# Pairing each group's values with the next group's scores in layer A, under a re-fitted order planner

## The chip, the cores and the metric

The kernel runs on one core of a Trainium2 chip. The time is device microseconds from one execution of the whole program. The core's engines each work through their own instruction list in order and meet through semaphores: PE (matrix multiply, with its weight loads shown apart as PEld), DVE (vector), ACT (activations and copies), POOL (masks and the weight loads' DMA issues) and SP (other DMA issues). Three timed runs of the kernel before took 1802.33, 1803.32 and 1803.51 us; the median is 1803.32 us. A change of 0.2% is 3.6 us.

## The reference

Two attention layers stand side by side, each on 2048 positions of width 1024, with 32 heads of 32:

```
qkv = x @ wqkv                                  # both layers
A: each query sees 8 keys, 2 positions apart    # window 8, dilation 2
B: each query sees its last 256 keys            # sliding block
p = softmax(q k / sqrt(32)) ;  o = p v
out = concat(o_A @ wo_A, o_B @ wo_B)
```

All inputs are float32. Nothing is left out or approximated by the change.

## The kernel before

The work is cut into eight units of 512 positions. Units 0 to 3 are layer B ("dense"); units 4 to 7 are layer A, whose positions the host has sorted into even and odd ones, so that the dilation disappears and each query sees its last 8 neighbours. In each unit the 32 heads make eight groups of four heads. Groups are counted through, `hg = 8 u + s`, so layer A has the groups 32 to 63.

Projections are exact to nearly float32: each operand is split into a high fp32r part and the remainder, and three products are summed. In the profile's rows `raw` is a freshly loaded float32 tile, `w`, `x` and `r` are split operands, `g` is the PSUM bank of a projection (three banks), `s` a bank of scores (four banks), `o` the bank of an attention output. The splits are done by `Stream.parts` (L243 to L256): a cast on ACT (L249) or DVE (L252), then subtractions on DVE (L255). Loads into `raw` are issued from POOL's queue (L194), and each waits until the split of an older tile has freed its buffer.

A dense group computes row maxima from a first pass of scores (L1356, L1361), then scores a second time with exponentials (L1441) and masks (L1420), then its values (`o<-pbuf,vbuf`). A group of layer A (`window`, L1145) does this:

- scores: 64 small matmuls of 32 rows by 32 columns, `s<-pbuf` in the rows; they are float32, so the profile counts 128. They read the group's queries and keys from a seat (two seats, L580) that SP's DMAs fill.
- the chain: mask on DVE (L1184), maximum and subtraction (L1194, L1196), exponential on ACT (L1200), sum, reciprocal, product and transpose on DVE (L1208 to L1214), and eight copies on ACT that spread the result into `wide` (L1223, L1226).
- values: 16 or 20 matmuls of 32 columns, `o<-wide,vbuf` (32 or 40 in the profile).

Layer A also forms its output projection and part of its value projection with seven block products in place of eight; the sums of inputs and weights for that are formed on DVE out of line (L1073, L1105), and partial results are gathered by `L979` and `L874`.

What decides the order of all this is a planner inside the kernel's Python. `Clock` holds a modelled time of each engine, of the port that DVE and POOL share, and of DMA transfers. Four lists wait for PE: `a` (small extras), `2` (second scores and values), `1` (first scores and layer A's scores) and `g` (projections, in a fixed sequence). At each step the item with the earliest ready time is issued (L1577 to L1610), and whatever hangs on its end (casts, splits, copies, DMA issues) is issued to the other engines when the model's time reaches it. So a changed number in `Clock` re-deals the instructions of every engine.

One more rule looks after the supply of PE's instructions, which the program gets in chunks of 256. `short(n)` (L299) says that a burst of `n` instructions would outrun what has been fetched; then a projection item is taken in place of the burst, if one is ready:

```
return ck.now < asked[1] + FETCHED and issued[0] + EXTRA + n > asked[0] * CHUNK + ASKED + LEFT
```

Of the kernel before, what the change touches and what calls it, by code (L numbers as in the profile page):

```python
# [22 lines left out]
ASK = 2  # L23
# [8 lines left out]
P_LATE = 1.5  # L32
VPARTS = ((0,4),(4,2),(6,2))
# [19 lines left out]
CW = 1.36  # L53
# [9 lines left out]
class Clock:  # L63
# [7 lines left out]
    MOVE = dict(load=(2.12, 0.14), store=(0.64, 0.4), copy=(1.18, 0.56),  # L71
# [3 lines left out]
    def __init__(self):  # L75
        self.free = dict(pe=0.0, act=0.0, dve=0.0, pool=0.0, sp=0.0)
        self.port = dict(dve=0.0, pool=0.0)
        self.later, self.lands, self.busy = [], [], []
        self.n = 0
# [17 lines left out]
    def use(self, eng, dur, *ready, port=False):  # L97
        end = self.free[eng] = self.ends(eng, dur, *ready, port=port)
        if eng == "pool" or port:
            self.port[eng] = end  # L100
        return end + self.SEEN[eng]

    def issue(self, eng, kind, *ready):
        start = max((self.free[eng],) + ready) + (0.28 if eng == "pool" else 0.0)
        self.free[eng] = start + self.HOLD[eng]
        return self.move(start + self.LEAD[eng], *self.MOVE[kind])

# [18 lines left out]
    def move(self, t, dur, tail):  # L126

        busy = self.busy = [x for x in self.busy if x[1] > self.now - 20.0]
        i = 0
        while i < len(busy):  # L130
            if busy[i][1] <= t or busy[i][0] < t:
                t = max(t, busy[i][1])
            elif busy[i][0] - t >= dur:
                break
            else:
                t = busy[i][1]
            i += 1
        busy.insert(i, (t, t + dur))
        return t + dur + tail
# [10 lines left out]
class Stream:  # L150
# [14 lines left out]
    def load_to(self, n):  # L165
        while not self.loaded:
# [4 lines left out]
            for n, (i, h) in enumerate(FIRST):  # L171
                raw, t = self.raw[i]
                ap = self.items[i][1]
                queue, took = (self.nc.scalar, self.ck.load) if n in BY_ACT else (self.nc.sync, self.ck.copy)
# [90 lines left out]
def kernel(ctx, tc, xs, wqk, wv, wo, outs, units):  # L265
# [33 lines left out]
    def short(n):  # L299
        return ck.now < asked[1] + FETCHED and issued[0] + EXTRA + n > asked[0] * CHUNK + ASKED + LEFT  # L300
# [27 lines left out]
    for k in ("stack", "v", "o", "ot", "out", "nat", "second", "clear", "scores", "s", "t", "vs", "vw", "vd"):  # L328
        done[k] = {}
# [210 lines left out]
    def qk_items(u, s):  # L540
# [14 lines left out]
        def evac_window(t, ps, bank):  # L555
# [5 lines left out]
            else:  # L561
# [5 lines left out]
                if u + 1 < U and not units[u + 1][3]:  # L567
                    ck.defer(e + 1.0, lambda: (nc.vector.memset(tails[:, s, :], 0.0), ck.use("dve", 0.08, ck.now)))
# [70 lines left out]
        for t in range(2):  # L639
# [15 lines left out]
            def run(k, t=t, h=h):  # L655
# [12 lines left out]
                if k == ASK and t == 0 and u > DU and kinds[:1] == ["x"] and st.split >= where["qk", u, s, 1]:  # L668
                    st.split_to(where["qk", u, s, 1] + 1)
# [30 lines left out]
    def v_items(u, part):  # L700
# [25 lines left out]
        def run(r, n, k, b):  # L726
# [418 lines left out]
    def window(u, s):  # L1145
# [100 lines left out]
        return [Item(scores_ready, scores, CW, 256)], [Item(values_ready, values, C3 + 0.9, 16 * len(kbs))]  # L1246
# [404 lines left out]
```

## Time and profile before

| | |
|---|---|
| median of three runs | 1803.32 us |
| the profiled execution | 1802.41 us, of which the span of instructions is 1800.7 us |
| mean granted PE clock | 0.999 |
| PE busy | 1775.3 us (99%) |
| DVE busy | 1297.4 us (72%) |
| ACT busy | 940.3 us (52%) |
| POOL busy | 413.7 us (23%) |
| DMA | 324.58 MB, mean 180 GB/s |

A row of the timeline gives the start, the length and the number of instructions of a run of equal ones; in brackets stands the idle time ahead of it and what ended that. A row of the waits gives, for an engine and line, the total, the number and the longest of its idle stretches by what released them; "issue" means that the instruction waited for nothing else that the profile shows. A matmul's row lasts longer than the step to the next one, since matmuls overlap; the step is what counts, and it is read from the starts.

### The profile page before, as it was taken

What the parts mean: (1) busy time and instruction counts of PE and PEld (TensorE: products, weight loads), DVE (VectorE), ACT (ScalarE), POOL (GpSimd) and SP (SyncE); (2) the same over time, 40 slices, a digit from 0 to 9 for tenths busy, and PEclk for the clock granted to TensorE, in tenths of its full rate; (3) what the DMA queues carried; (4) which work ended last, traced back from release to release, by engine and by line L of the source; (5) the groups of instructions that cost most, each with busy time, mean ns of one, the idle gap of its engine ahead of it and who ended that gap; (6) DMA issues with size and microseconds to landing.
All of it is one profiled execution on the core that took longest, in us unless ns stands there. A gap on an engine that the chain in (4) does not pass through costs nothing.

```text
span 1800.7 us, 38453 instructions
## 1 busy us (share of the span) xinstructions
PE 1775.3 (99%) x14496; PEld 1439.2 (80%) x14496; DVE 1297.4 (72%) x2887; ACT 940.3 (52%) x2336; POOL 413.7 (23%) x952
## 2 busy tenths in 40 slices
PE   9999999999999999999999999999999999999999
PEld 7787777888777888778788778877888787778887
DVE  6777876768867769867678566756666768688866
ACT  4565566555656565655655444534454435355442
POOL 3222323222242222332223400110011101001120
PEclk9999999999999999999999999999999999999999
DMA  8354664644645555455546265665466558758984
GB/s 245 112 152 135 185 167 135 171 138 138 185 141 172 152 131 167 144 159 148 141 124 174 84 190 180 213 211 187 160 212 204 192 177 285 265 181 273 350 287 146
DMA packets 154794, 324.58 MB, mean 180 GB/s; under 512 B 18032, under 2 KB 58992, under 8 KB 154608
## 3 DMA queue, kind: packets, MB, share of 16 engines
q0 software_dynamic: 45792, 166.74, 29.8%
q1 hardware_dynamic: 98736, 137.02, 26.6%
q10 hardware_dynamic: 10080, 18.35, 2.7%
q8 instruction: 115, 1.88, 0.4%
q14 instruction: 71, 0.58, 0.1%
HBM read 201.33 MB, written 53.48 MB: 142 GB/s over the span
## 4 chain that ended last, share of the span: by engine, by line
PE 87%; DVE 5%; issue 3%; DMA 2%; ACT 2%; POOL 1%; DVEq 0%; POOLq 0%; ACTq 0%
PE g L297 68%; PE s L297 13%; PE o L297 6%; DMA raw<-xs 1%; DVE w L255 1%; DVE x L255 1%; ACT s L1361 0%; DVE band L1212 0%; DMA raw<-wv 0%; DVE sm L1208 0%; DVE band L1184 0%; ACT w L249 0%; DMA raw<-wqk 0%; DVE w L252 0%; DMA qst<-nat 0%
## 5 line engine op out<-in xcount | busy, mean ns | idle before, releaser
L297 PE MATMUL g<-x,w 128*128 128x512 f32 x3552 | 878.9, 393 | 5.0 <-DVE x L255 3.9
L297 PEld LDWEIGHTS g<-x,w 128*128 128x128 f32 x3552 | 654.8, 188 | 135.2 <-issue 6.6
L255 DVE TENSOR_TENSOR w<-raw,w 128x512 fp32r<-128x512 f32 x510 | 334.3, 697 | 48.5 <-ACT w L249 42.4
L1361 ACT ACTIVATE s<-s,nm 128x384 f32<-128x384 f32 (+2 forms) x512 | 274.4, 537 | 108.2 <-DVE nm L1356 101.7
L1356 DVE CUSTOM_DVE_ANT_0 s<-s,mask_d 128x384 f32<-128x384 f32 (+2 forms) x512 | 261.7, 553 | 91.7 <-PE s L297 91.4
L297 PE MATMUL g<-w,x 128*128 128x256 f32 (+1 forms) x1728 | 307.9, 327 | 2.4 <-DVE w L255 1.5
L1420 POOL TENSOR_SCALAR_AFFINE_SELECT pbuf<-pbuf 128x128 f32<-128x128 f32 (+1 forms) x603 | 218.4, 390 | 317.9 <-ACT pbuf L1441 315.9
L297 PEld LDWEIGHTS g<-w,x 128*128 128x128 f32 x1728 | 255.2, 190 | 28.0 <-DVE w L255 2.8
L297 PE MATMUL g<-r,w 128*128 128x512 f32 x960 | 239.0, 393 | 1.7 <-issue 1.2
L1441 ACT ACTIVATE pbuf<-s 128x384 f32<-128x384 f32 (+2 forms) x480 | 203.1, 505 | 64.2 <-PE s L297 62.0
L297 PEld LDWEIGHTS g<-r,w 128*128 128x128 f32 x960 | 177.2, 188 | 37.2 <-issue 2.0
L194 POOL DMA_DIRECT2D raw<-wqk x126 | 68.6, 544 | 407.4 <-DVE w L255 256.8
L297 PEld LDWEIGHTS s<-qst,kst 128*128 128x128 f32 x704 | 113.4, 188 | 42.6 <-ACT s L1361 16.8
L297 PE MATMUL s<-kst,qst 96*128 96x384 f32 (+2 forms) x512 | 142.6, 342 | 0.9 <-ACT s L1361 0.7
L297 PE MATMUL s<-qst,kst 128*128 128x256 f32 (+2 forms) x704 | 137.0, 302 | 4.0 <-ACT s L1361 3.2
L252 DVE CAST w<-raw 128x1024 fp32r<-128x1024 f32 x173 | 119.8, 692 | 19.3 <-PE g L297 9.0
L249 ACT CAST w<-raw 128x1024 fp32r<-128x1024 f32 (+1 forms) x83 | 85.8, 1038 | 71.1 <-PE g L297 29.7
L297 PEld LDWEIGHTS s<-kst,qst 96*128 96x128 f32 x512 | 93.6, 189 | 26.3 <-issue 4.4
L1361 ACT ACTIVATION_READ_ACCUMULATOR s<-s,nm 128x1 f32 x512 | 105.3, 206 | 0.0
L1223 ACT COPY wide<-band 32x512 f32<-32x512 f32 x128 | 79.0, 617 | 31.0 <-DVE band L1214 29.4
L297 PE MATMUL o<-pbuf,vbuf 128*32 128x384 f32 (+2 forms) x1408 | 91.2, 388 | 0.0
L597 ACT ACTIVATE nat<-g 128x512 fp32r<-128x512 f32 x64 | 38.3, 598 | 98.2 <-PE g L297 89.0
(90 smaller groups left out, 1432.1 us busy)
## 6 DMA issues: line engine op xcount, KB each, us to landing
raw<-wqk POOLq DMA_DIRECT2D x126, 512.0 KB, 4.6
raw<-wv POOLq DMA_DIRECT2D x60, 512.0 KB, 5.0
qst<-nat SPq DMA_DIRECT2D x96, 256.0 KB, 5.7
kst<-nat SPq DMA_DIRECT2D x96, 256.0 KB, 5.7
raw<-wo POOLq DMA_DIRECT2D x44, 512.0 KB, 4.4
raw<-xs POOLq DMA_DIRECT2D x28, 512.0 KB, 4.5
outs<-ost ACTq DMA_DIRECT2D x38, 256.0 KB, 3.1
kst<-halo SPq DMA_DIRECT2D x72, 128.0 KB, 4.5
```

The costliest lines, as they stand in the source:

```text
L194: (self.nc.scalar if early else self.nc.gpsimd).dma_start(raw if len(ap.shape) == 2 else raw.rearrange("p (a b) -> p a b", a=2), ap)
L249: nc.scalar.copy(t[:, 0, :], raw)
L252: nc.vector.tensor_copy(t[:, 0, :], raw)
L255: nc.vector.tensor_tensor(t[:, 1, c:c + 512], raw[:, c:c + 512], t[:, 0, c:c + 512].bitcast(F32), op=ALU.subtract)
L297: nc.tensor.matmul(out, left, right, **k)
L597: nc.scalar.activation(hl[:, 0, :], ps, AF.Copy, scale=sc)
L1223: nc.scalar.copy(diag[r:r + 32, :, :, c:c + 32], turned[r:r + 32, :, :, 1, :])
L1356: nc.vector.tensor_tensor_reduce(ps[:, :n], ps[:, :n], mask[:, cut:full], scale=-1.0, scalar=BIG, op0=ALU.add, op1=ALU.min, accum_out=nm)
L1361: nc.scalar.activation(ps[:, :n], ps[:, :n], AF.Exp, bias=nm, scale=-1.0, accum_out=sm)
L1420: nc.gpsimd.affine_select(w, w, pattern=[[0, m], [step, n]], compare_op=ALU.is_ge, fill=0.0, base=base, channel_multiplier=chan)
L1441: nc.scalar.activation(w, ps[:, :pack * n].rearrange("p (j n) -> p j n", j=pack), AF.Exp)
```

## The change

The change has six parts.

1. In layer A, for the groups 33 to 49 (`PAIRED = 50`), a group's scores are held until the previous group's spread probabilities are modelled as there (plus `P_LATE`), and the values of the previous group are held until those scores have been issued. So the two stand together on PE. The scores count, for `short`, with the values' instructions too.
2. `short` also limits a burst once the last asked chunk has come: then one more chunk counts as there.
3. The model of the shared port keeps the stretches in which DVE holds it, and POOL waits only if it starts inside one.
4. The model of DMA keeps two streams, one for loads from POOL's queue and one for the rest. They share the bandwidth where they overlap, and a load takes 1.5 + 0.76 in place of 2.12 + 0.14.
5. In the start, a loop variable had the name of the function's argument, so that eight items were wanted at once; it has another name now, and six are wanted.
6. Smaller: the eight clears of `tails` go from DVE to POOL; the split of a unit's second key weights ahead of its inputs is also made for the dense units 2 and 3; in the wide value items two weight tiles are wanted ahead in place of one.

```diff
+PAIRED = 50
...
-    MOVE = dict(load=(2.12, 0.14), store=(0.64, 0.4), copy=(1.18, 0.56),
+    MOVE = dict(load=(1.5, 0.76), store=(0.64, 0.4), copy=(1.18, 0.56),
...
         if eng == "pool":
-            t = max(t + 0.06, self.port["dve"])
-        elif port:
-            t = max(t, self.port["pool"])
-        return t
+            t += 0.06
+            return next((e for s, e in self.held if s <= t < e), t)
+        return max(t, self.port) if port else t
...
-    def move(self, t, dur, tail):
...
+    def move(self, eng, t, dur, tail):
+
+        mine, other = self.moves[eng == "pool"], self.moves[eng != "pool"]
+        t = begin = max(t, mine[-1][1] if mine else 0.0)
+        for s, e in other:
+            if e <= t:
+                continue
+            n = max(s - t, 0.0)
+            if n >= dur:
+                break
+            t, dur = t + n, dur - n
+            n = min((e - t) / 2, dur)
+            t, dur = t + 2 * n, dur - n
+            if not dur:
+                break
+        mine.append((begin, t + dur))
...
-            for n, (i, h) in enumerate(FIRST):
+            for turn, (i, h) in enumerate(FIRST):
...
     def short(n):
-        return ck.now < asked[1] + FETCHED and issued[0] + EXTRA + n > asked[0] * CHUNK + ASKED + LEFT
+        there = asked[0] * CHUNK + ASKED + LEFT + (0 if ck.now < asked[1] + FETCHED else CHUNK)
+        return issued[0] + EXTRA + n > there
...
-                    ck.defer(e + 1.0, lambda: (nc.vector.memset(tails[:, s, :], 0.0), ck.use("dve", 0.08, ck.now)))
+                    ck.defer(e + 1.0, lambda: (nc.gpsimd.memset(tails[:, s, :], 0.0), ck.use("pool", 0.08, ck.now)))
...
-                if k == ASK and t == 0 and u > DU and kinds[:1] == ["x"] and st.split >= where["qk", u, s, 1]:
+                if k == ASK and t == 0 and u > 1 and kinds[:1] == ["x"] and st.split >= where["qk", u, s, 1]:
...
-                    ahead(item_of(n + 1))
+                    ahead(item_of(min(n + 2, 3)))
...
         def scores_ready():
-            return latest(rs.empty(), done["stack"].get((u, s)),
+            if last_dense + 1 < hg < PAIRED and hg - 1 not in done["p"]:
+                return None
+            return latest(rs.empty(), done["stack"].get((u, s)), done["p"][hg - 1] + P_LATE if last_dense + 1 < hg < PAIRED else 0.0,
...
-                h["p"] = ck.use("act", 0.31, e)
+                done["p"][hg] = h["p"] = ck.use("act", 0.31, e)
...
         def values_ready():
+            if hg + 1 < PAIRED and hg + 1 not in done["scores"]:
+                return None
...
-        return [Item(scores_ready, scores, CW, 256)], [Item(values_ready, values, C3 + 0.9, 16 * len(kbs))]
+        return [Item(scores_ready, scores, CW, 256 + (16 * len(kbs) if hg < PAIRED else 0))], [Item(values_ready, values, C3 + 0.9, 16 * len(kbs))]
```

Matmuls and DMA issues are the same in number and kind as before; a few casts, copies and masks go from one engine to another. Where they all stand is another matter. On PE, at the start of layer A, before (`s<-pbuf` are scores, `o<-wide,vbuf` values, `g` projections):

```order
L297 MATMUL s<-pbuf 32x40 x64
L297 MATMUL g<-x,w 128x512 x27
L297 MATMUL s<-pbuf 32x40 x64
L297 MATMUL g<-x,w 128x512 x18
L297 MATMUL g<-r,w 128x512 x15
L297 MATMUL o<-wide,vbuf_131 32x136 x12
L297 MATMUL o<-wide,vbuf_131 32x128 x4
L297 MATMUL s<-pbuf 32x40 x64
```

and in the changed kernel, from its second group of layer A on:

```order
L303 MATMUL s<-pbuf 32x40 x64
L303 MATMUL o<-wide,vbuf_127 32x136 x12
L303 MATMUL o<-wide,vbuf_127 32x128 x4
L303 MATMUL g<-x,w 128x512 x69
L303 MATMUL g<-w,x 128x256 x42
L303 MATMUL s<-pbuf 32x40 x64
L303 MATMUL o<-wide,vbuf_127 32x136 x12
L303 MATMUL o<-wide,vbuf_127 32x128 x4
```

Scores and values touch at 4 places of the 32 groups before, and at 18 now; between one such pair and the next stand 57 to 114 projection matmuls.

On POOL, at the program's start, before (the selects build the masks):

```order
L194 DMA raw<-wqk 128x1024 x2
L463 MEMSET keep_d 128x128
L464 ISA
L464 AFFINE_SELECT ident<-keep_d 128x128
L467 MEMSET pick 32x16
L469 AFFINE_SELECT pick<-pick 32x16 x2
```

and now, with the end of the masks and what follows them:

```order
L462 MEMSET keep_f 128x128
L464 AFFINE_SELECT keep_f<-keep_f 128x128
L462 MEMSET keep_d 128x128
L464 AFFINE_SELECT keep_d<-keep_d 128x128
L200 DMA raw<-wqk 128x1024 x2
L200 DMA raw<-wv 128x2x512 x5
```

The masks have gone ahead of the first two weight loads; the five value-weight loads, which stood behind the masks in the kernel before too, follow at once.

On DVE, around the splits of the last unit's inputs (`x<-raw,x`, two instructions for each of four loads), before:

```order
L255 TENSOR_TENSOR x<-raw,x 128x512 x2
L979 TENSOR_TENSOR r<-g,r 128x512 x2
L1208 TENSOR_REDUCE sm<-band 128x16
L1210 RECIPROCAL sm<-sm 128x16
L1212 TENSOR_TENSOR band<-band,sm 128x16x40
L1214 STREAM_TRANSPOSE band<-band 128x1024
L1184 TENSOR_TENSOR band<-s,near 128x4x40 x4
L255 TENSOR_TENSOR x<-raw,x 128x512 x2
```

and now:

```order
L261 TENSOR_TENSOR x<-raw,x 128x512 x2
L1217 TENSOR_REDUCE sm<-band 128x16
L1219 RECIPROCAL sm<-sm 128x16
L1221 TENSOR_TENSOR band<-band,sm 128x16x40
L1223 STREAM_TRANSPOSE band<-band 128x1024
L986 TENSOR_TENSOR r<-g,r 128x512 x2
L261 TENSOR_TENSOR x<-raw,x 128x512 x2
L986 TENSOR_TENSOR r<-g,r 128x512 x2
L261 TENSOR_TENSOR x<-raw,x 128x512 x2
L1193 TENSOR_TENSOR band<-s,near 128x4x40 x4
```

The chain of one group has gone from between the third and the fourth pair of splits to between the second and the third, and the next group's masks (L1184, now L1193) have gone behind the fourth.

More of the change, by code (lines that the diff above doesn't have):

```diff
@@ L76, in __init__ @@
         self.free = dict(pe=0.0, act=0.0, dve=0.0, pool=0.0, sp=0.0)
-        self.port = dict(dve=0.0, pool=0.0)
-        self.later, self.lands, self.busy = [], [], []
+        self.port, self.held = 0.0, []
+        self.later, self.lands, self.moves = [], [], [[], []]
         self.n = 0
@@ L98, in use @@
         end = self.free[eng] = self.ends(eng, dur, *ready, port=port)
-        if eng == "pool" or port:
-            self.port[eng] = end
+        if eng == "pool":
+            self.port = end
+        elif port:
+            self.held = [x for x in self.held if x[1] > self.now - 5.0] + [(end - dur, end)]
         return end + self.SEEN[eng]
@@ L105, in issue @@
         self.free[eng] = start + self.HOLD[eng]
-        return self.move(start + self.LEAD[eng], *self.MOVE[kind])
+        return self.move(eng, start + self.LEAD[eng], *self.MOVE[kind])
     def copy(self, kind, *ready):
@@ L170, in load_to @@
                 self.raw[3 + i] = raw, [None, None]
-            for n, (i, h) in enumerate(FIRST):
+            for turn, (i, h) in enumerate(FIRST):
                 raw, t = self.raw[i]
                 ap = self.items[i][1]
-                queue, took = (self.nc.scalar, self.ck.load) if n in BY_ACT else (self.nc.sync, self.ck.copy)
+                queue, took = (self.nc.scalar, self.ck.load) if turn in BY_ACT else (self.nc.sync, self.ck.copy)
                 if h is None:
@@ L327 @@
     done = {}
-    for k in ("stack", "v", "o", "ot", "out", "nat", "second", "clear", "scores", "s", "t", "vs", "vw", "vd"):
+    for k in ("stack", "v", "o", "ot", "out", "nat", "second", "clear", "scores", "s", "t", "vs", "vw", "vd", "p"):
         done[k] = {}
```

11 lines of the change are left out of this document (1 added, 10 removed).

## The prediction

> **What bounds the kernel now.** I read the page first, for who is busy.
>
> ```profile
> span 1800.7 us, 38453 instructions
> PE 1775.3 (99%) x14496; PEld 1439.2 (80%) x14496; DVE 1297.4 (72%) x2887; ACT 940.3 (52%) x2336; POOL 413.7 (23%) x952
> ```
>
> PE is the bound from end to end. The change adds no matmul and takes none away, so it can move the time in two ways only: by PE's idle stretches, and by the dearer steps where PE goes from 128-column to 32-column matmuls and back. So the second view is PE's own waits.
>
> ```profile
> PE s L297 <- ACT s L1361: 4.6, 7, 1.0
> PE g L297 <- DVE x L255: 3.9, 3, 2.8
> PE g L297 <- DVE w L255: 3.0, 6, 0.8
> PE s L297 <- issue: 2.2, 1, 2.2
> PE g L297 <- DVE w L252: 1.5, 2, 1.0
> PE s L297 <- DVE qst L1569: 1.5, 1, 1.5
> PE g L297 <- issue: 1.2, 1, 1.2
> PE s L297 <- DVE hl L1382: 0.6, 2, 0.3
> PE s L297 <- DVE qst L1396: 0.6, 2, 0.4
> ```
>
> These nine rows make 19.1 us, 1.1% of the span (smaller ones are left out). That is about all that a new order can win; what it can lose has no such ceiling. Most of these waits are single events, so I looked each up in the timeline and then asked the built order whether the instructions that made it still stand so.
>
> **The change part by part.** *Pairing.* Two stretches of PE's timeline, first values alone, then values right behind scores:
>
> ```profile
> 1156.53 10.50 PE L297 MATMUL g<-x,w 128*128 128x512 f32 x45
> 1166.87 1.52 PE L297 MATMUL g<-w,x 128*128 128x512 f32 x6
> 1168.32 1.12 PE L297 MATMUL o<-wide,vbuf 128*32 128x136 f32 x32
> 1169.37 0.50 PE L297 MATMUL g<-w,x 128*128 128x512 f32 x1
> ...
> 1177.06 1.32 PE L297 MATMUL s<-pbuf 32*32 32x40 f32 x128
> 1178.31 1.12 PE L297 MATMUL o<-wide,vbuf 128*32 128x136 f32 x32
> 1179.36 0.96 PE L297 MATMUL g<-w,x 128*128 128x512 f32 x3
> ```
>
> A projection steps in (1166.87 - 1156.53) / 45 = 0.23 us. The six ahead of the lone values took 1168.32 - 1166.87 = 1.45, so the last of them, which leads into 32-column work, took 1.45 - 5 x 0.23 = 0.30, with the rounding up to 0.32: 0.09 dearer at most. The values' own 1.05 is the same alone (1169.37 - 1168.32) and behind scores (1179.36 - 1178.31). So a pair saves one entry and nothing else. Scores and values touch at 18 places now and touched at 4: 14 x 0.09 = **-1.3 us**; the ends are that and, if a pair has a cost of its own, 0. The new wait is the planner's and stands in no queue: PE does projections meanwhile. What it holds up is the seat that SP's DMAs fill for the next group but one; the pairs stand 57 to 114 projections apart (13 to 26 us), which leaves that room. Behind the last values of the built order stand 537 matmuls (123 us), so a layer A that ends a little later costs nothing. I cost this at zero; without that cover it would be a wait of PE for the seat, as long as the slip.
>
> *The supply of instructions.* The page's row of the queue that brings them (packets, MB, share), and PE's timeline at the longest wait on "issue":
>
> ```profile
> q8 instruction: 115, 1.88, 0.4%
> 1046.76 1.32 PE L297 MATMUL s<-pbuf 32*32 32x40 f32 x128
> 1054.36 1.24 PE L297 MATMUL s<-pbuf 32*32 32x40 f32 x119
> 1057.76 0.28 PE L297 MATMUL s<-pbuf 32*32 32x40 f32 x9 [2.17 <-issue]
> ```
>
> 1.88 MB in 115 packets are 16 KB each, one for about 256 of PE's 29,000 instructions (each matmul has its weight load). A projection phase needs one packet in 29 us, but a group of scores uses 256 instructions in 1.2 us. The second group here came 7.6 us behind the first and ran dry after 119 of 128. The "issue" rows above make 3.4 us. A pair uses 320 or 336 instructions at once, which is worse, but no pair now follows another within 13 us, and `short` refuses more. The groups from 50 on still stand freely, so I keep 0.6: **-2.8 us**. The ends are -3.4 and, if pairs run dry, the first rival.
>
> *The start.* POOL's first rows, DVE's wait for the value weights, DVE beside the longest select, and PE's first use of the first weight load:
>
> ```profile
> 8.70 0.68 POOL L194 DMA_DIRECT2D raw<-wqk  x1 [8.19 <-DVE x L255]
> 10.74 3.83 POOL L464 TENSOR_SCALAR_AFFINE_SELECT ident<-keep_d 128x128 fp32r<-128x128 f32 x1
> 22.93 2.19 POOL L194 DMA_DIRECT2D raw<-wv  x3
> 30.55 0.69 DVE L252 CAST w<-raw 128x1024 fp32r<-128x1024 f32 x1 [7.10 <-DMA raw<-wv]
> 10.72 1.29 DVE L255 TENSOR_TENSOR r<-pbuf,r 128x512 fp32r<-128x512 f32 x2
> 12.52 1.29 DVE L255 TENSOR_TENSOR r<-pbuf,r 128x512 fp32r<-128x512 f32 x2
> 19.69 2.88 PE L297 MATMUL g<-x,w 128*128 128x512 f32 x12
> ```
>
> POOL's list was blocked for 8.2 us by a load whose buffer was not free, the masks came behind it, and the value weights were issued at 22.93; PE then waited 0.6 (DVE w L252) and 0.8 (DVE w L255, its longest) for them. With the masks first (some 12.4 us of work, from just ahead of 10.74 to 22.93), the loads go out from about 13 us, two for the first weights and then the value weights, some 8 us earlier than now. Those 1.4 us go. In turn the first weight load moves from 8.70 to about 13 and its data, first needed at 19.69 by the projection in the last row, come 4 us later, and masks run beside DVE's first splits; for both I put 0.3: **-1.1 us**, with ends -1.4 and +1.5 (the wait moved to the first load, as long as the one removed).
>
> [...] In the rows above DVE's two-input splits kept their 0.6 us each inside POOL's 3.83 us select, so here it was at most POOL that waited. [...]
>
> *The dense units.* PE's waits between 440 and 970 us, and one of them in the timeline:
>
> ```profile
> PE s L297 <- ACT s L1361: 1.8, 3, 0.6
> PE s L297 <- DVE hl L1382: 0.6, 2, 0.3
> PE g L297 <- DVE r L1320: 0.4, 2, 0.2
> ...
> 453.14 0.82 PE L297 MATMUL s<-qst,kst 128*128 128x128 f32 x4 [0.61 <-ACT s L1361]
> ```
>
> Two or three times each, so one event for each unit from the second on. At 453.14 nine score matmuls stood in a row, filling five banks where there are four, so the last pairs wait for the exponential of the first. In the built order such rows of five banks are cut by three projections (0.7 us), which is more than the 0.61. I take 2.2 of these 2.8 us off. In the first unit the other 2.8 us of the same row (4.6 - 1.8) come from runs of scores with nothing to put between; the new order has the same kind of runs there, a little looser: 1.0 off. Together **-3.2 us**, ends -5.6 and 0.
>
> *The last unit's inputs.* DVE around PE's longest wait (2.8, DVE x L255):
>
> ```profile
> 1511.59 1.28 DVE L979 TENSOR_TENSOR r<-g,r 128x512 f32<-128x512 f32 x2
> 1514.76 1.29 DVE L255 TENSOR_TENSOR x<-raw,x 128x512 fp32r<-128x512 f32 x2 [1.88 <-ACT x L249]
> 1517.17 0.81 DVE L1208 TENSOR_REDUCE sm<-band 128x16 f32<-128x640 f32 x1
> 1521.22 1.27 DVE L255 TENSOR_TENSOR x<-raw,x 128x512 fp32r<-128x512 f32 x2
> ```
>
> From 1517.17 to 1521.22 DVE did a group's chain and the next one's masks, 4.05 us, while PE waited for the splits behind them. In the built order the chain stands a load earlier, where DVE had 1.88 us to spare, and the masks behind the splits. So the splits come 1.88 + 0.9 (the masks) earlier: **-2.4 us** of 2.8, ends -2.8 and 0.
>
> *A weight behind sums.* Also on DVE:
>
> ```profile
> 1431.59 1.79 DVE L1073 TENSOR_TENSOR r<-r 128x256 f32<-128x256 f32 x4
> 1433.30 0.69 DVE L252 CAST w<-raw 128x1024 fp32r<-128x1024 f32 x1
> ```
>
> PE waited 1.0 (DVE w L252) and 0.8 (DVE w L255) for this cast and the splits behind it. In the built order the cast and its splits stand ahead of the four sums, 1.7 us earlier: **-1.7 us**, ends -1.8 and 0.
>
> *What is late next.* The clear of `tails` on POOL and the other small edits move single instructions of 0.1 us on engines with room, and cost nothing. But each engine's order is dealt anew, and waits that no row of before shows will come. I put them at a third of what the last three terms give back, 7.3 / 3 = **+2.4 us**; the ends are 0 and all 7.3, since the same hand could be dealt again.
>
> The sum is -1.3 - 1.1 - 2.8 - 3.2 - 2.4 - 1.7 + 2.4 = -10.1 us. The profiled execution took 1802.4 us, its span and 1.7 us around it; 1802.4 - 10.1 = 1792.3. It lay 0.9 under the median of the three runs, so I predict 1793.2 us. With all good ends it is -1.4 - 1.4 - 3.4 - 5.6 - 2.8 - 1.8 = -16.4, so 1787; with all bad ones 1.5 + 7.3 = +8.8, so 1812.
>
> **The rivals.** *Pairs run dry* (slower). Each of the 17 pairs holds up to 336 instructions; if a pair begins before the packet asked for during the last one is there, PE stands for some 2.2 us, as at 1057.76. For it: the count of instructions that `short` goes by was fitted to the old order. Against it: the spacing. Five stalling pairs eat the forecast's gain; ten give 1793.2 + 10 x 2.2 = 1815 us.
>
> *The same hand again* (no change). What is gained in the places that I looked up is lost in others: the dense, input and weight terms give nothing in all, and the new waits come on top, -1.3 - 1.1 - 2.8 + 2.4 = -2.8, so 1800.5 us, 0.16% under before. For it: all those waits are accidents of an order, and the model that deals has changed, not what the kernel needs. Against it: they can be named, and each stands better now.
>
> [...]
>
> **How the numbers follow.** The three runs before lie within 0.07%; 0.2%, 3.6 us, is about what can be told from no change. Forecast 0.70; masks hold the start 0.04; same hand 0.12; pairs run dry 0.10; 0.04 for a worse deal that I don't see. So faster 0.74, same 0.12, slower 0.14. The forecast's own range is 1787 to 1799. To leave out no more than 2 in 10, the range takes in the same hand: 1787 to 1803.
>
> **What would show it.** Pairing: no wait on "issue" over 1 us before group 50, values right behind scores with a 1.25 us step. The start: value weights issued near 14 us and no PE wait near 31 us. Dense: the waits for ACT s L1361 fall from 4.6 us to about 2.4. Inputs: the longest wait for DVE x L255 under 1 us. PE's waits in all near 11 us. I am wrong if "issue" rows grow, if a wait for x or w over 2 us stands at another unit's start, or if the gap between first and last PE instruction shrinks by less than 6 us.

## The result, and the profile after

The change made the kernel slower: median 1810.22 us in eight runs, beside 1803.67 us for the kernel before in eight; the ratio is 1.0033, with a 95% interval of 1.0019 to 1.0046. The profiled execution took 1809.79 us. The page of the changed kernel begins:

```profile
span 1808.1 us, 38431 instructions
PE 1777.1 (98%) x14496; PEld 1441.7 (80%) x14496; DVE 1300.2 (72%) x2871; ACT 935.3 (52%) x2326; POOL 422.7 (23%) x978
q8 instruction: 115, 1.88, 0.4%
```

The span is 7.4 us longer with as many matmuls. PE's waits, over the whole span:

```profile
PE s L303 <- ACT s L1372: 6.7, 9, 2.1
PE g L303 <- DVE band L881: 5.6, 2, 3.9
PE g L303 <- DVE w L261: 4.5, 9, 1.3
PE o L303 <- issue: 1.9, 2, 1.5
PE s L303 <- DVE qst L1580: 1.5, 1, 1.5
PE s L303 <- ACT ln L1385: 1.1, 1, 1.1
...
PE g L303 <- DVE x L261: 0.2, 1, 0.2
```

Some rows did what was forecast: the wait for x is 0.2 us where it was 3.9, the longest wait for a weight's second split (w L261) is one of 1.3 us, "issue" in all is 1.9. Others grew: the wait for ACT's exponentials (6.7, was 4.6), and a new one of 5.6 us for the adds of the output products (L881, which was L874 and 0.3 us before).

For a sum by stage, each step from one PE matmul to the next was set against the usual one: the 20th percentile of such a pair of shapes over all kernels of this study. What lies above it is called lost time; it holds the waits, the half-clock steps (below) and all small delays, which are most of it: PE's named waits are 20.7 us in all before and 25.0 after.

| us | before | after | difference |
|---|---|---|---|
| usual steps in all (fewer entries into 32-column work) | 1621.9 | 1620.3 | -1.6 |
| lost: start, 0 to 40 us | 6.2 | 4.2 | -2.0 |
| lost: the rest of the first unit, to 440 | 37.3 | 38.9 | +1.6 |
| lost: second to fourth dense unit, 440 to 1040 | 47.8 | 55.2 | +7.4 |
| lost: layer A, 1040 to 1640 | 77.7 | 69.3 | -8.4 |
| lost: end of layer A and what follows | 3.7 | 14.3 | +10.6 |
| first to last matmul | 1794.7 | 1802.1 | +7.4 |

(The rows are rounded.) So layer A, the start and the entries gained 12.0 us. The dense units, the first one included, for which the forecast had -3.2, and the end, for which it had nothing of its own, lost 19.6.

**The dense units.** PE's waits from 440 to 1040 us, where the kernel before had 2.8 us in all:

```profile
PE s L303 <- ACT s L1372: 4.5, 5, 2.1
PE g L303 <- DVE w L261: 1.1, 1, 1.1
PE s L303 <- ACT ln L1385: 1.1, 1, 1.1
PE s L303 <- DVE hl L1393: 0.6, 1, 0.6
```

The longest of them, on three engines (PE first, then DVE, then ACT):

```profile
965.16 2.23 PE L303 MATMUL g<-x,w 128*128 128x512 f32 x9
969.53 1.01 PE L303 MATMUL s<-kst,qst 96*128 96x384 f32 x2 [2.15 <-ACT s L1372]
...
965.42 0.43 DVE L258 CAST x<-raw 128x512 fp32r<-128x512 f32 x1 [4.29 <-PE g L303]
965.89 0.69 DVE L261 TENSOR_TENSOR x<-raw,x 128x512 fp32r<-128x512 f32 x1
...
967.56 0.68 DVE L1331 TENSOR_TENSOR r<-o,r 128x512 fp32r<-128x512 f32 x1
968.16 0.56 DVE L1367 CUSTOM_DVE_ANT_0 s<-s,mask_d 128x384 f32<-128x384 f32 x1
...
968.81 0.56 ACT L1372 ACTIVATE s<-s,nm 128x384 f32<-128x384 f32 x1 [2.86 <-DVE nm L1367]
```

DVE stood for 4.29 us at a cast that waited for PE's projections to be done with its tile. The row maxima (L1367) were queued behind it, ACT's exponential waited for them, and PE for the bank. No engine was short of time; the order was wrong by a few instructions.

**The end of layer A.** DVE, then PE, then the stretch in which the granted clock fell (columns: stretch, length, busy time and count of PE, PEld, DVE, ACT, POOL, PE clock, DMA share, GB/s):

```profile
1651.97 1.01 DVE L1193 TENSOR_TENSOR band<-s,near 128x160 f32<-128x160 f32 x4
1657.87 2.87 DVE L1112 TENSOR_TENSOR r<-r 128x512 f32<-128x512 f32 x4 [4.89 <-DMA r<-od]
1660.65 0.68 DVE L881 TENSOR_TENSOR ost<-g,r 128x512 f32<-128x512 f32 x1
...
1674.96 0.69 DVE L881 TENSOR_TENSOR band<-g,r 128x512 f32<-128x512 f32 x1 [2.90 <-DMA outs<-band]
...
1666.08 5.82 PE L303 MATMUL g<-x,w 128*128 128x512 f32 x24 [1.67 <-DVE band L881]
1675.80 5.09 PE L303 MATMUL g<-x,w 128*128 128x512 f32 x15 [3.90 <-DVE band L881]
1680.82 1.18 PE L303 MATMUL o<-wide,vbuf 128*32 128x8 f32 x40
```

```profile
1660.00:1680.00 20.00, 13.87 (x52) 10.33 (x51) 16.83 (x27) 9.60 (x16) 2.12 (x4) 0.91 0.92 321
```

DVE stood 4.89 us at the sums for the output products (L1112), whose loads had not landed; everything behind them came late: the chain of layer A's last group, the splits, and the adds (L881) that free PE's three banks. One of those adds then waited 2.90 us for the store of an earlier add, itself among the late ones. PE waited 1.67 and 3.90 us, and its granted clock was 0.50 for 3.41 us from 1675.42: the 15 projections from 1675.80 to 1680.82 took 0.33 us each, not 0.23. In all PE waited 8.1 us behind 1640 us, where the kernel before had 0.3: 6.1 for the adds (0.56 of it for one with another output, `ost`), 1.5 on "issue" and 0.5 for a DMA.

**Layer A.** A pair on PE, and PE's two waits on issue:

```profile
1155.24 10.39 PE L303 MATMUL g<-x,w 128*128 128x512 f32 x45
1165.56 1.32 PE L303 MATMUL s<-pbuf 32*32 32x40 f32 x128
1166.80 1.12 PE L303 MATMUL o<-wide,vbuf 128*32 128x136 f32 x32
1167.86 0.96 PE L303 MATMUL g<-x,w 128*128 128x512 f32 x3
...
1501.29 0.42 PE L303 MATMUL o<-wide,vbuf 128*32 128x128 f32 x6 [0.40 <-issue]
1651.36 0.41 PE L303 MATMUL o<-wide,vbuf 128*32 128x128 f32 x4 [1.50 <-issue]
```

Scores step in 1.24 us, values in 1.06, and no pair ran dry. The two rows on "issue" are of groups behind the 50th, which still stand freely.

**The start.** The select that took 3.83 us before, and POOL's first loads, where before the value weights were issued at 22.93:

```profile
1.09 0.29 POOL L471 TENSOR_SCALAR_AFFINE_SELECT ident<-keep_d 128x128 fp32r<-128x128 f32 x1
9.98 1.23 POOL L200 DMA_DIRECT2D raw<-wqk  x2
11.29 0.72 POOL L200 DMA_DIRECT2D raw<-wv  x1
16.28 0.73 POOL L200 DMA_DIRECT2D raw<-wv  x1 [4.28 <-DVE w L261]
```

PE no longer waits near 31 us. The select took 0.29 us here, ahead of DVE's splits, and 3.83 us in the kernel before, beside them, while the splits kept their 0.6 us each. So it was POOL that had waited, and the masks were done by 9.98 us, not by about 13. The port that the two engines share is a term of the planner's model; of it the traces show such lengths and no more.

### The profile page after: what moved, and what is told of

Same layout as the page of the kernel before. It is cut to its first block, busy times and chain, and to the rows that moved or that the text cites. A ratio compares the mean times of both kernels' runs of the same rounds, so it can differ in the third digit from the quotient of the medians.

```text
span 1808.1 us, 38431 instructions
## 1 busy us (share of the span) xinstructions
PE 1777.1 (98%) x14496; PEld 1441.7 (80%) x14496; DVE 1300.2 (72%) x2871; ACT 935.3 (52%) x2326; POOL 422.7 (23%) x978
## 4 chain that ended last, share of the span: by engine, by line
PE 82%; DVE 7%; DMA 6%; issue 2%; ACT 2%; POOL 1%; SPq 0%; ACTq 0%; DVEq 0%; POOLq 0%
PE g L303 64%; PE s L303 12%; PE o L303 6%; DMA raw<-xs 2%; DVE w L261 2%; DMA r<-od 1%; DVE s L1367 1%; DVE x L261 1%; ACT s L1372 1%; POOL pbuf L1431 1%; DMA raw<-tv 1%; DVE w L258 1%; DMA sd<-r 1%; DMA outs<-band 0%; DMA od<-r 0%
## 5 line engine op out<-in xcount | busy, mean ns | idle before, releaser
L303 PEld LDWEIGHTS g<-x,w 128*128 128x128 f32 x3552 | 658.7, 188 | 136.4 <-issue 10.1
L261 DVE TENSOR_TENSOR w<-raw,w 128x512 fp32r<-128x512 f32 x510 | 337.0, 702 | 42.6 <-ACT w L255 36.4
L1367 DVE CUSTOM_DVE_ANT_0 s<-s,mask_d 128x384 f32<-128x384 f32 (+2 forms) x512 | 261.7, 555 | 118.3 <-PE s L303 117.5
L1431 POOL TENSOR_SCALAR_AFFINE_SELECT pbuf<-pbuf 128x128 f32<-128x128 f32 (+1 forms) x621 | 230.1, 398 | 269.4 <-ACT pbuf L1452 267.0
L1193 DVE TENSOR_TENSOR band<-s,near 128x160 f32<-128x160 f32 x128 | 32.5, 317 | 90.0 <-PE s L303 90.0
L200 POOL DMA_DIRECT2D raw<-wv x60 | 38.7, 645 | 233.9 <-DVE w L261 122.0
```

The lines of the kernel that those rows point to most:

```text
L200: (self.nc.scalar if early else self.nc.gpsimd).dma_start(raw if len(ap.shape) == 2 else raw.rearrange("p (a b) -> p a b", a=2), ap)
L261: nc.vector.tensor_tensor(t[:, 1, c:c + 512], raw[:, c:c + 512], t[:, 0, c:c + 512].bitcast(F32), op=ALU.subtract)
L303: nc.tensor.matmul(out, left, right, **k)
L1193: nc.vector.tensor_tensor(p64()[:, j, :, 24:], banks[j][0][:, :160].rearrange("p (b c) -> p b c", b=4), m, op=ALU.add)
L1367: nc.vector.tensor_tensor_reduce(ps[:, :n], ps[:, :n], mask[:, cut:full], scale=-1.0, scalar=BIG, op0=ALU.add, op1=ALU.min, accum_out=nm)
L1431: nc.gpsimd.affine_select(w, w, pattern=[[0, m], [step, n]], compare_op=ALU.is_ge, fill=0.0, base=base, channel_multiplier=chan)
```

## Experiments

Each kernel is the kernel before with some of the change's parts: P pairing, L the new limit for supply, R the renamed variable, C the clears on POOL, T two tiles ahead, E the early splits of units 2 and 3, Mp the model of the port, Mt the model of transfers. "All" is the changed kernel. The ratio is to the kernel before, measured beside it. The kernel before had medians from 1803.15 to 1804.35 us on these occasions. The columns by stage and "half", the number of windows of 3.41 us that PE ran at half clock, are from the one profiled execution, which lies up to 4.5 us from the median.

| kernel | median us | ratio, 95% | lost: start | to 440 | dense | layer A | end | half |
|---|---|---|---|---|---|---|---|---|
| before | 1803.67 | | 6.2 | 37.3 | 47.8 | 77.7 | 3.7 | 1 |
| all | 1810.22 | 1.0019-1.0046 | 4.2 | 38.9 | 55.2 | 69.3 | 14.3 | 1 |
| all but P | 1815.72 | 1.0053-1.0086 | 4.2 | 39.8 | 54.2 | 75.1 | 16.1 | 5 |
| P | 1806.26 | 1.0009-1.0029 | 6.3 | 38.9 | 47.5 | 79.9 | 7.7 | 2 |
| P L R C T E | 1807.40 | 1.0007-1.0027 | 4.6 | 37.6 | 59.5 | 72.4 | 6.8 | 5 |
| Mp Mt | 1824.20 | 1.0095-1.0131 | 6.9 | 39.7 | 59.7 | 72.0 | 15.3 | 6 |
| all, sums later | 1806.89 | 1.0014-1.0035 | 4.2 | 38.9 | 54.5 | 71.7 | 8.7 | 1 |
| Mt | 1827.06 | 1.0107-1.0138 | 9.9 | 41.2 | 55.2 | 78.1 | 14.1 | 6 |
| Mp | 1817.30 | 1.0056-1.0091 | 7.4 | 39.4 | 58.1 | 72.3 | 15.1 | 5 |
| P L R C T | 1801.12 | 0.9973-0.9991 | 4.6 | 37.4 | 52.6 | 75.8 | 3.7 | 2 |
| all but E | 1819.58 | 1.0073-1.0101 | 4.3 | 39.6 | 56.9 | 71.6 | 14.9 | 4 |
| before, nudged up | 1810.09 | 1.0024-1.0049 | 6.2 | 42.3 | 54.4 | 72.1 | 7.3 | 4 |
| before, nudged down | 1816.84 | 1.0062-1.0089 | 5.4 | 45.5 | 54.9 | 75.8 | 6.0 | 4 |
| all, nudged up | 1810.26 | 1.0029-1.0055 | 4.1 | 41.4 | 55.6 | 70.0 | 10.5 | 3 |
| nudged up, P | 1824.86 | 1.0097-1.0128 | 5.5 | 41.1 | 55.9 | 81.8 | 10.1 | 5 |
| nudged down, P | 1820.31 | 1.0070-1.0100 | 8.2 | 44.6 | 55.1 | 76.1 | 7.2 | 3 |
| P L | 1803.36 | 0.9984-1.0005 | 6.2 | 38.9 | 47.5 | 74.6 | 6.4 | 2 |
| P L R C T, nudged up | 1809.84 | 1.0022-1.0042 | 4.8 | 38.8 | 55.2 | 74.0 | 5.5 | 2 |
| P L T | 1802.97 | 0.9992-1.0010 | 5.7 | 37.4 | 53.8 | 72.6 | 3.8 | 1 |
| R | 1800.91 | 0.9977-1.0000 | 4.6 | 37.4 | 47.5 | 77.5 | 4.2 | 1 |

**The large parts, taken out and alone.** The pairing out of the changed kernel, and alone in the kernel before:

```diff
+            if last_dense + 1 < hg < PAIRED and hg - 1 not in done["p"]:
+                return None
...
+            if hg + 1 < PAIRED and hg + 1 not in done["scores"]:
+                return None
...
-        return [Item(scores_ready, scores, CW, 256)], [Item(values_ready, values, C3 + 0.9, 16 * len(kbs))]
+        return [Item(scores_ready, scores, CW, 256 + (16 * len(kbs) if hg < PAIRED else 0))], [Item(values_ready, values, C3 + 0.9, 16 * len(kbs))]
```

> The changed kernel with all its parts but the pairing (the two conditions, and the values counted with the scores for the supply of instructions, are out). If the pairing cost the time (theory 1: it ties every group to the chain of the one before, layer A comes out later and its end runs into the output products), the loss goes: about 1799 to 1802 us, PE's waits for L881 near the end under 1 us. If the new model of port and DMA cost it (theory 2: it re-deals the dense units and the end of layer A worse), the loss stays and the 1.3 us of the pairing and some of the supply come on top: 1810 to 1814 us, waits between 440 and 1040 us about 7 us as in the changed kernel. If no single part cost it (theory 3: every change of a number deals all engines anew, and the parts do not add), it lies anywhere from 1797 to 1812.

> The kernel before with the pairing alone. Theory 1: about 1808 to 1812 us, slower than before by the loss seen. Theory 2: faster than before by the pairing's 1.3 us and by the 3.4 us of waits on issue, 1798 to 1801 us. Theory 3: neither is bound to hold; the dense units, which stand ahead of every pair, should keep their waits to the last row, and the difference should lie behind 980 us alone.

Then the models of port and transfers as before in the changed kernel, and alone in the kernel before:

```diff
-    MOVE = dict(load=(2.12, 0.14), store=(0.64, 0.4), copy=(1.18, 0.56),
+    MOVE = dict(load=(1.5, 0.76), store=(0.64, 0.4), copy=(1.18, 0.56),
...
-            t = max(t + 0.06, self.port["dve"])
+            t += 0.06
+            return next((e for s, e in self.held if s <= t < e), t)
...
-    def move(self, t, dur, tail):
+    def move(self, eng, t, dur, tail):
```

> The changed kernel with the model of port and DMA as before (and the load at 2.12 + 0.14), all else kept. Theory 1: still about 1808 to 1812 us. Theory 2: 1796 to 1801 us, PE's waits from 440 to 1040 us back at about 2.8 us. Theory 3: any of 1797 to 1812, with losses in places that stand in no other kernel.

> The kernel before with the new model of port and DMA alone (and the load at 1.5 + 0.76). Theory 1: 1799 to 1804 us. Theory 2: 1808 to 1814 us, with about 7 us of PE's waits from 440 to 1040 us and a wait for L874 (the adds of the output products) of some 5 us near the end. Theory 3: a time in between, and waits in other places than in the changed kernel.

Measured: 1815.72, 1806.26, 1807.40 and 1824.20 us. The first theory, that the pairing cost it, falls: without it the changed kernel is 5.5 us slower still. The second holds for the direction only: the models cost 2.8 us on top of the other parts (1810.22 - 1807.40) and 19.9 alone. And the parts do not add: the pairing saves 5.5 us in one place and costs 1.9 in the other. Alone it also ran dry, which it did not in the changed kernel. PE's waits on "issue" behind 1040 us with the pairing alone:

```profile
PE g L298 <- issue: 2.1, 3, 1.0
PE o L298 <- issue: 2.7, 3, 1.5
PE s L298 <- issue: 0.9, 2, 0.6
```

**The end of layer A alone.** The sums are dealt to DVE later, which can move nothing ahead of 1640 us:

```diff
-        ck.defer(e + (BG_EARLY if key == "s" and who[0] < PAIRS[0] else BG_SLACK), add)
+        ck.defer(e + (BG_EARLY if key == "s" else BG_SLACK), add)
```

> The changed kernel; only the sums that feed the last unit's output products are put into DVE's order 8 us behind their loads' modelled landing, in place of 1.5 us. Nothing ahead of about 1640 us can move. If the model of the transfers lets the loads land too early (theory 2), so that DVE stands in front of the sums while the adds that free PE's banks queue behind it, the two waits for L881 (5.6 us) fall under 2 us and with them the half-clock stretch at 1676 us: 1803 to 1806 us. If the transfers are simply full there, L881 still waits, for the stores of its own band: 1809 to 1811 us.

Measured 1806.89 us, 3.3 less than the changed kernel; the end's lost time went from 14.3 to 8.7. Between 1640 us and the end PE waited in one place for those adds, and the half-clock stretch was gone (the 21 projections step in 0.24 us):

```profile
1673.40 5.02 PE L303 MATMUL g<-x,w 128*128 128x512 f32 x21 [2.78 <-DVE band L881]
1678.35 1.18 PE L303 MATMUL o<-wide,vbuf 128*32 128x8 f32 x40
```

So the sums that came too early made about half of the end's loss (5.6 of 10.6 us). Of the 5.0 us left, this trace's waits behind 1640 us name 4.4: the 2.78 above, 1.35 on "issue" and 0.30 for a DMA. The add that PE waited 2.78 us for stood in DVE's list behind the next sums (2.86 us) and the chain of the last group, and DVE worked there without a break from 1664.85 to 1673.17 us. The wait was to fall under 2 us, and the time is 0.9 us over the range that the theory gave: the theory holds for a part.

**The two models apart.** With the two numbers of the load, the transfers alone; then the port alone.

> The kernel before with the new model of transfers alone (two streams, and the load at 1.5 + 0.76). If the loss of the new models lies in the transfers: 1812 to 1824 us, with waits for L874 near the end of 4 us or more and a wait for DMA kst<-nat at the start. If it lies in the port: 1802 to 1807 us.

> The kernel before with the new model of the port alone. If the loss of the new models lies in the transfers: 1801 to 1806 us, L874 waits under 1 us. If it lies in the port (POOL's work modelled as starting earlier, so masks and loads put where they can't run yet): 1812 to 1824 us, with PE waits in the dense units of 6 us or more.

Measured 1827.06 and 1817.30 us: the question was put wrongly, since both lose. But the wait for the adds at the end tells them apart. From 1640 us on, with the transfers alone and with the port alone:

```profile
PE g L301 <- DVE band L878: 3.5, 2, 3.0
```

```profile
PE s L298 <- issue: 4.5, 1, 4.5
PE g L298 <- DVE band L875: 0.6, 1, 0.6
```

All six kernels dealt with the new model of transfers wait 3.9 to 6.1 us in all for these adds (the seventh, with the sums later, 2.8); of the others, and of the kernel before, none waits over 0.6 us. That wait therefore goes with the model of transfers. The port's kernel lost as much at the end by another accident, a group of scores that ran dry for 4.49 us.

**The early splits.** The changed kernel under the old models, without the splits ahead of units 2 and 3, and then the changed kernel without them:

```diff
-                if k == ASK and t == 0 and u > 1 and kinds[:1] == ["x"] and st.split >= where["qk", u, s, 1]:
+                if k == ASK and t == 0 and u > DU and kinds[:1] == ["x"] and st.split >= where["qk", u, s, 1]:
```

> The kernel before with the pairing, the new limit for supply, the renamed variable, the clears on POOL and the two tiles ahead; the models of port and transfers, and the splits ahead of units 2 and 3, as before. If those early splits cost the 5.7 us for hl L1388 between 440 and 1040 us that the kernel with the old models showed (and the four half-clock windows with them): 1796 to 1800 us, which is faster than both kernels. If they were not the cause: 1805 to 1809 us, with the same two waits of 2.9 us.

> The changed kernel without the early splits of units 2 and 3 alone. If those splits cost time by themselves, as they did under the old models (6.3 us): about 1804 us, PE's waits from 440 to 1040 us at about 3 us. If they cost it there only through the order that the old models dealt, and the new models carry the loss: 1808 to 1812 us. If the order is a lottery (theory 3): anything from 1802 to 1820.

Measured 1801.12 and 1819.58 us. Under the old models the same line costs 6.3 us, under the new ones leaving it out costs 9.4. It has no price of its own. The first of these two is faster than both kernels (0.9982, 0.9973 to 0.9991).

**A nudge that says nothing.** One number, 0.01 us:

```diff
-    SEEN = dict(act=0.15, dve=0.115, pool=0.08)
+    SEEN = dict(act=0.16, dve=0.115, pool=0.08)
```

> The kernel before with one number of the model that says nothing new: a result of ACT is taken as seen 0.16 us after its end in place of 0.15 us. If orders follow what a model knows (theories 1 and 2): 1802 to 1806 us, no change that can be measured. If every re-dealt order is a new draw, and the order of before a picked one (theory 3): slower by the 5 to 20 us that the single parts showed, with waits in new places.

> The same nudge the other way, 0.14 us. Theories 1 and 2: 1802 to 1806 us. Theory 3: another draw, 1808 to 1825 us, and not the same distance as with 0.16.

> The changed kernel with the same nudge, 0.16 us. Theories 1 and 2: 1809 to 1812 us, no change. Theory 3: another draw; if the order of the changed kernel is a picked one too, 1813 to 1830 us, and if it is not, as easily faster as slower.

Measured 1810.09, 1816.84 and 1810.26 us. The kernel before loses 6.8 us with 0.16 and 13.5 with 0.14, as much as the whole change cost (6.5), and twice that; the changed one keeps its time, though by another order: its end loses 3.8 us less, its first unit 2.5 more. The loss of the first nudged kernel lies in the dense units and at the end. Its waits from 440 to 1040 us, and PE around 212 us, where it ran at half clock (the three projections step in 0.43 us from 212.60 to 213.88):

```profile
PE s L297 <- DVE hl L1382: 4.1, 2, 2.1
PE s L297 <- ACT s L1361: 1.8, 3, 0.6
```

```profile
212.11 0.69 PE L297 MATMUL s<-kst,qst 96*128 96x384 f32 x1 [0.73 <-ACT s L1361]
212.60 1.48 PE L297 MATMUL g<-x,w 128*128 128x512 f32 x3
213.88 0.52 PE L297 MATMUL s<-kst,qst 96*128 96x384 f32 x1
```

**The pairing on other orders, and the limit.**

> The kernel before nudged to 0.16 us (1810.1 us), and the pairing alone on top. The pairing cost 1.9 us on the order of before and saved 5.5 us on the changed one. If it saves by itself (fewer entries into 32-column work, less running dry): 1804 to 1809 us. If it costs by itself: 1811 to 1815 us. If what is seen is the new draw: either sign, by 3 us or more.

> The kernel before nudged to 0.14 us (1816.8 us), and the pairing alone on top. As above: 1811 to 1816 us if the pairing saves by itself, 1818 to 1822 us if it costs, either sign by 3 us or more if it is the draw.

> The kernel before with the pairing and the new limit for the supply of instructions. With the old limit the pairs ran dry: PE's waits on issue were 5.7 us where before had 3.7. If the new limit is what keeps them supplied in the changed kernel (issue 1.9 us, none above 0.5 us ahead of group 50): issue under 2 us in all, and if nothing else moves 1802 to 1804 us. If the spacing of the pairs did it: issue stays near 5 us.

> The fastest kernel so far (1801.1 us: pairing, new limit, renamed variable, clears on POOL, two tiles ahead, old models) with ACT seen after 0.16 us. If its parts are worth their 3 us by themselves: 1799 to 1804 us. If it owes them to a lucky draw: 1806 to 1818 us, as the nudges did to the kernel before.

Measured 1824.86, 1820.31, 1803.36 and 1809.84 us. On four orders the pairing moved the time by +1.9, +14.8, +3.5 and -5.5 us. The first three have the old limit and the last has the new one, so the sizes show the draw, and the sign may be the limit's; the limit alone was not run. With the pairing and no new limit layer A loses 76.1 to 81.8 us (three kernels), with both 69.3 to 75.8 (nine), without the pairing 72.0 to 78.1 (eight). Not all of this need be the limit's, since most of the nine have other parts too. The clean pair is the pairing without the limit and with it: 79.9 and 74.6 us, and from 1040 to 1640 us the waits on "issue" of the kernel with both are

```profile
PE s L298 <- issue: 0.2, 1, 0.2
```

With the old limit the pairs also broke up: scores and values touch at 12 places, with the new limit at 19. So the limit keeps the pairs supplied; the spacing, which the prediction had leaned on, did not do it alone (with the old limit the pairs stand 48 to 123 projections apart). One more wait on issue, of 1.4 us, stands behind 1640, so the 2 us expected were not exceeded. In time the pairing with its limit is worth nothing that can be measured: the ratio is 0.9995 (0.9984 to 1.0005), since of what layer A and the entries gain, 2.7 us come back at the end, and 1.6 in the first unit, where the order is that of before but a window at half clock fell. The faster kernel owes its 3 us largely to its draw: nudged, it is at 1809.84, beside 1810.09 for the kernel before with the same nudge.

**The dense units kept, and the start alone.**

```diff
-            for n, (i, h) in enumerate(FIRST):
+            for turn, (i, h) in enumerate(FIRST):
...
-                queue, took = (self.nc.scalar, self.ck.load) if n in BY_ACT else (self.nc.sync, self.ck.copy)
+                queue, took = (self.nc.scalar, self.ck.load) if turn in BY_ACT else (self.nc.sync, self.ck.copy)
```

> The kernel before with the three parts that touch only layer A: the pairing, the new limit and the two tiles ahead. The dense units keep the order of before, so PE's waits from 440 to 1040 us must stay at 2.8 us. If the dense units are where a new draw costs most, and layer A's parts gain: 1797 to 1803 us. If layer A's draw decides as much: up to 1810 us.

> The kernel before with the renamed variable alone, so that the start wants six tiles in place of eight. Its own gain is at the start: PE's waits up to 40 us fall from 3.3 to about 2 us. But the start re-deals all that follows it: if the order of the dense units in before is one good draw, the waits from 440 to 1040 us go from 2.8 to 6 us or more, and the time to 1806 to 1816 us. If the gain stands alone: 1801 to 1803 us.

Measured 1802.97 and 1800.91 us. The first missed its aim: the two tiles ahead touch the value items of the dense units as well, whose waits went to 7.7 us and whose lost time to 53.8. Beside the kernel without the two tiles (P L), which has the same median within 0.4 us, the first unit, layer A and the end lose 6.1 us less and make up for that. The second came out as if the gain stood alone: PE's order is that of the kernel before, row for row, and only other engines' differ; the start loses 4.6 in place of 6.2 us, and from 440 to 1040 us PE waits as in the kernel before:

```profile
PE s L297 <- ACT s L1361: 1.8, 3, 0.6
PE s L297 <- DVE hl L1382: 0.6, 2, 0.3
PE g L297 <- DVE r L1320: 0.4, 2, 0.2
```

The ratio of this kernel is 0.9989 (0.9977 to 1.0000), so the gain is at the edge of what can be told from none.

## Why the prediction was wrong

The forecast was 1793.2 us, 10 under the kernel before; it came out 6.5 over. The steps, by the profiled executions:

- **Pairing, -1.3.** Right: the entries into 32-column work went from 60 to 46 and the usual steps fell by 1.6 us, no pair waited on issue, and values step in 1.06 us. "Pairs run dry" did not come; that the spacing forbids it was the wrong reason, the new limit does.
- **Supply, -2.8.** Waits on "issue" went from 3.7 to 1.9 us, so -1.8; the two that stayed are in groups behind the 50th, where 0.6 had been kept and 1.9 came.
- **Start, -1.1.** Lost time fell by 2.0 us; the renamed variable alone gave 1.6. The masks' 12.4 us, read from the kernel before, held POOL's own waiting; they took 9.2 us, and the loads went out at 9.98 us, not at about 13.
- **Inputs, -2.4, and weight, -1.7.** The wait for x fell from 3.9 to 0.2 us. The cast did go ahead of the sums, and its two waits went. But waits for weights between 1040 and 1600 us did not fall in all (3.6 before, 4.2 now), so the weight's -1.7 came back as others. Layer A as a whole lost 8.4 us less; the three terms on its waits had 6.9. A half-clock window that followed those two waits in the kernel before went with them, some 1.6 us for which no term stood.
- **The dense units, -3.2: the step that failed.** "In the built order such rows of five banks are cut by three projections ... I take 2.2 of these 2.8 us off." The cut was there, and no first score waited for a bank from 440 to 1040 us; but second scores did, five times, 4.5 us in all. The waits of the second to fourth dense unit rose from 2.8 to 7.3 us, the lost time by 7.4; the first unit, with 1.0 off, lost 1.6 more. I looked up the places where before had waited, and a new order waits elsewhere. The runs show how one-sided this is: four kernels have PE's order of before in those units (before, P, P L and R), and lose 47.5 to 47.8 us there; the other sixteen, with eleven other orders, lose 52.6 to 59.7, whatever was changed, a number by 0.01 us included. Kernels with one and the same order there lie within 1.5 us. The order of before is the best of those seen here, and every change that touched it gave it up.
- **"So a layer A that ends a little later costs nothing", and "the ends are 0 and all 7.3": the second failure.** The matmuls behind the last values were no cover, because DVE, not PE, stood in the way: the sums for the output products were dealt too close behind their loads. +10.6 us, against which stood only the +2.4 for all waits that no row shows. The wait for the adds, 6.1 us here, stands in every kernel that has the model of transfers (2.8 to 6.1); a free group that ran dry took 1.5 us, and one window at half clock came on top. The ceiling of 7.3 us on new waits had no row behind it; they are not bounded by what the removed ones were worth, as the prediction had said itself ("what it can lose has no such ceiling"). The second to fourth dense unit and the end together brought 18.0.
- **The rivals.** "The same hand again" had the right mechanism, that waits are accidents of an order, and too small a price (-2.8 in all). "A worse deal that I don't see" had a chance of 0.04; of the nineteen other kernels that were timed, thirteen are slower than before by over 0.2% and none faster by as much. "Masks hold the start" had a chance of 0.04, the author's estimate; that a select keeps DVE from a split as long as it runs was not shown. The first select took 0.29 us, ahead of the splits; beside the later ones a split took at most 0.84 us in place of 0.68, and the start lost 2.0 us less.

What stays open: why the order of before is so good in the dense units, and how much of the loss at the end that remains with the sums later is also owed to the model of transfers. That a better order of layer A under the new models exists together with the old dense order was not tried.

## What to carry to other kernels

Where a model deals the order of everything, any edit to it is first of all a new draw, and only then the gain that it was made for: nudge a number that means nothing by a hundredth and time that, before an edit's effect is believed. Nudge it both ways, since one nudge can come out even, as the changed kernel's did. If the nudges cost more than the edit gains, the order is likely a picked one, and an edit is worth trying first where it leaves the picked stretches as they are, as the one renamed variable did. And when pricing such a change, don't only ask whether the old waits are gone: walk down each in-order queue for the instruction that will stand on a late operand, and count who is behind it.

## What the runs showed of the hardware

A wait can be paid twice. In the kernel before PE's granted clock was 0.50 from 1435.65 to 1439.06 us and 1.00 in the 3.41 us on either side, of which the one ahead had lost 2.2 us to two waits for a weight (0.97 and 0.77) and small delays. In all twenty profiled executions the half-clock stretches between the first and the last matmul are 3.41 us long or twice that, and lie on a grid of 3.41 us that is placed anew in each. For each window of the grid that was not itself at half clock, the lost time in it was set against the next window:

| lost in a window | next one at half clock, windows without 32-column matmuls | the same, windows with 32-column matmuls |
|---|---|---|
| 2.2 us or more | 34 of 34 | 5 of 19 |
| 1.65 to 2.2 us | 18 of 83 | 0 of 126 |
| less | 0 of 8908 | 0 of 1268 |

The 63 windows at half clock lost 1.7 us on average, where the median window lost 0.1; so one costs some 1.6 us. By that estimate a wait of 2 us that falls into one window costs up to 3.6, the same wait across two windows 2. The longest wait of the kernel before, 2.78 us, lay across two, which lost 2.0 and 1.8 us with a wait of 0.52 behind it; the granted clock stayed at 1.00. Windows at half clock are a good part of the draws' price: the two nudged kernels before have four such windows each, the kernel before one. They also shift one and the same order from one execution to the next: of 23 executions of the kernel before beside the first experiments, the five under 1801.5 us had a mean granted clock of 0.999 or 1.0, the nine over 1805 us 0.997 or 0.998.

In 45 of the 57 windows with one at half clock behind them, PE lost less than 2.7 us of the 3.41, and worked in the rest of it.
